# Two units of the RWKV5 attention go over to the 64-step form, and the 64-step form turns its blocks before it moves them

## The chip, the core and the metric

The kernel runs on one core of one Trainium2 chip. The core has a matrix engine (PE, TensorE), a vector engine (DVE, VectorE), a scalar engine (ACT), a general engine (POOL, GpSimd) and an engine that here only issues DMAs (SP, SyncE). Each engine takes its instructions in program order and waits for the others by semaphores. The metric is the device time of one execution in microseconds (us), the median of three timed runs.

## The reference

Batch 4, 8 heads, 768 steps, head dimension 48. An RWKV5 attention runs over the steps; its output, seen as 3072 tokens of 384 values, feeds a SwiGLU feed-forward block with 1536 hidden values.

```python
for t in range(S):
    kt, vt, rt = (k[:, :, t], v[:, :, t], r[:, :, t])
    cur = np.einsum('bhd,bhe->bhde', u[None] * kt, vt)
    y[:, :, t] = np.einsum('bhd,bhde->bhe', rt, state + cur)
    state = w[None, :, :, None] * state + np.einsum('bhd,bhe->bhde', kt, vt)
...
g = x @ w_gate
silu = g * (1.0 / (1.0 + np.exp(-g)))
val = x @ w_val
return (silu * val @ w_out)
```

## The kernel before

The attention is cut into 24 units of 128 rows. A unit `i` is either one batch and 128 steps (below `PAIRED`, here 0 to 9) or a pair of batches with 64 steps each (10 to 23). In a unit POOL scales k and r by powers of w (`scale_k`, `scale_r`) into slots of one large tile, `hats`. The scaled k and r must then be turned, so that the head dimension lies along the partitions, for the scores (k by r within the unit). `outputs` multiplies the masked scores (tile `At`, with the own term of u on the diagonal) by v and adds what the state of the earlier steps gives; `update` adds the unit's k by v to the state. `At` gets its masked scores from VectorE, by predicated copies.

*128-step units* are turned by TensorE: eight transposes of 128x128 into PSUM (`turn`, L415), which ACT copies to tiles `kT` and `rT`. Then come eight matmuls of scores (L508), the outputs (L659) and the update (L672); VectorE adds the update to the state `zs` (L684) and POOL multiplies that by w.

*64-step units* are turned without TensorE. `move_blocks` issues eight DMAs on SP (L445), which bring 32x32 blocks of `hats` to their partitions in slots 6 and 7 of `hats`, in runs of 32 values (128 bytes). Two transposes by VectorE (`turn_block`, L467), which turn each block of 32x32 within itself, then write `kT` and `rT`. Scores (L560) and outputs (L594) work on halves of 64 rows; the state lies beside v in `v_ld`, and two DMAs by SP (`fill_turned`, L538) bring the turned r into `At` for the outputs, and two by ACT (`fill_own`) the own term. `paired_update` (L608) comes right behind the scores of the next unit.

A loop over stages `s` sets the order. In stage s: POOL scales unit s + 1, units below 10 are turned, the scores of unit s − 1 come, and the outputs of unit s − 2 with their update: ahead of the scores for 64-step units, behind them for the last 128-step units (`LATE`). `after_visit` lists VectorE's small work of a 64-step stage in the deque `lazy`: masked copies, the own term, the two transposes of unit s, and the additions to the state. In the second transpose's step also stand the scaling of r and the moves of unit s + 1, the fills and the loads of unit s + 3. So the moves of a unit are issued a stage ahead of its transposes.

Between these, `gaps(s, n)` puts pieces of other work at five places of a stage, n from 0 to 4. From stage 12 they are pieces of the feed-forward block, as many as `share` says. In stages 4 to 11 the table `EARLY` lists them: `F` is a `feed`, one piece of the feed-forward block (there a gate group, `gate_value`, L705: six matmuls of 128x256 that serve two units, then a sigmoid on ACT and a product on VectorE, L712) with up to three steps of `lazy`. `R` is a `round_weights`: ACT and VectorE round a chunk of the weights (L214, L229), POOL completes it, and SP loads another chunk of 768 KB into `w_bits` (L194). Two PSUM banks serve the gate groups in turn, and two the rounding.

```python
    EARLY = {s: ("" if s < 7 else "R", "F", "R", "F", "RF") for s in range(5, 12)}
    EARLY[10] = ("", "FF", "RR", "F", "RF")
    EARLY[11] = ("R", "FF", "R", "F", "RF")
```

The loads, the moves and the fills stand on SP's one queue in program order, and each DMA there takes its turn on one of eight completion semaphores.

## Time and profile before

| | |
|---|---|
| median of 3 timed runs | 580.44 us (580.26 to 580.53) |
| the profiled execution | 579.8 us |
| its span on the core | 578.0 us |
| granted TensorE clock | 0.998 |
| instructions in the span | 13726 |

The profile's page gives the busy time of each engine, then 40 slices of the span, the DMA queues, the chain of work that ended last, and groups of instructions. The prediction quotes the lines that it uses. TensorE's row in the 40 slices reads 9 (90% or more) in all but the first and the last:

```profile
PE   8999999999999999999999999999999999999996
DVE  8887887299497699497789597878268787477772
DMA  8999895544544516534425534310200000200002
```

A row of a timeline has start, duration, engine, line, operation, out<-in, shapes and count. TensorE's rows count each float32 matmul of the program twice (a gate group of six reads x12), its transposes once.

### The profile page before, as it was taken

The page shows a single profiled execution, that of the slowest core. Times are in us where ns is not written, and L with a number is a line of the kernel's source. Part 1 is how long each engine was busy: PE and PEld are TensorE (multiplying, and loading weights), DVE is VectorE, ACT ScalarE, POOL GpSimd, SP SyncE. Part 2 cuts the span into 40 slices and gives each one's busy share as a digit, 9 for nine tenths or more (in the row PEclk, how much of TensorE's full clock was granted, in tenths as well). Part 3 has the DMA queues.
Part 4 walks back from the last instruction along what each step waited for, and adds up shares of the span by engine and source line. Part 5 has one row for each costly group of instructions (what it writes and reads, how often), then busy time and mean ns, then how long its engine had stood idle before and what let it go on. Part 6 is the DMA issues. An engine that isn't in the chain of part 4 may idle for free.

```text
span 578.0 us, 13726 instructions
## 1 busy us (share of the span) xinstructions
PE 569.0 (98%) x5424; PEld 512.8 (89%) x5424; DVE 428.4 (74%) x753; ACT 223.2 (39%) x532; POOL 394.4 (68%) x395
## 2 busy tenths in 40 slices
PE   8999999999999999999999999999999999999996
PEld 7788888899878899988899988899988899888896
DVE  8887887299497699497789597878268787477772
ACT  3768887222344432353521344421233320234310
POOL 6889898998999818979527979528988950010700
PEclk9999999999999999999999999999999999999999
DMA  8999895544544516534425534310200000200002
GB/s 203 239 262 260 229 238 113 113 70 102 106 84 84 95 29 127 109 64 94 77 40 105 120 69 78 56 35 20 56 1 0 1 1 2 54 2 0 2 1 59
DMA packets 152663, 49.16 MB, mean 85 GB/s; under 512 B 139729, under 2 KB 142802, under 8 KB 152594
## 3 DMA queue, kind: packets, MB, share of 16 engines
q1 hardware_dynamic: 147794, 41.22, 34.1%
q10 hardware_dynamic: 4800, 7.02, 4.4%
q8 instruction: 44, 0.72, 0.5%
q14 instruction: 25, 0.20, 0.1%
HBM read 28.31 MB, written 4.72 MB: 57 GB/s over the span
## 4 chain that ended last, share of the span: by engine, by line
PE 93%; POOL 2%; DMA 1%; SPq 1%; DVE 1%; issue 1%; ACT 0%; DVEq 0%; POOLq 0%
PE bank L974 30%; PE bank L785 18%; PE ring L974 13%; PE bank L705 11%; PE bank L1207 8%; PE ring L659 3%; PE ring L594 2%; PE ring L560 2%; PE ring L508 2%; PE ring L1207 1%; PE ring L415 1%; PE ring L608 1%; SPq L445 1%; DMA hats<-in_r_dram 1%; POOL rk L274 1%
## 5 line engine op out<-in xcount | busy, mean ns | idle before, releaser
L998 DVE TENSOR_TENSOR hv<-hv,bank 128x512 f32<-128x512 f32 x132 | 87.7, 683 | 40.4 <-PE bank L974 34.8
L705 PE MATMUL bank<-xT,wgv 128*128 128x256 f32 x288 | 66.2, 384 | 0.2 <-ACT xT L663 0.2
L974 PE MATMUL bank<-xf,wgv 128*128 128x256 f32 x256 | 65.8, 381 | 0.1
L998 ACT COPY hv<-bank 128x512 f32<-128x512 f32 x72 | 40.8, 584 | 58.8 <-PE bank L974 56.8
L705 PEld LDWEIGHTS bank<-xT,wgv 128*128 128x128 f32 x288 | 53.4, 190 | 8.2 <-ACT xT L663 0.4
L974 PEld LDWEIGHTS bank<-xf,wgv 128*128 128x128 f32 x256 | 47.9, 190 | 7.2 <-DVE kT L1252 0.6
L1261 POOL TENSOR_TENSOR hv<-At,hats 128x512 f32<-128x512 f32 x8 | 10.2, 1276 | 63.7 <-ACT At L1260 63.7
L1005 ACT ACTIVATE hv<-hv 128x512 f32<-128x512 f32 (+2 forms) x36 | 22.8, 633 | 52.8 <-DVE hv L998 52.8
L974 PE MATMUL bank<-xT,wgv 128*128 128x256 f32 x144 | 35.8, 381 | 0.0
L974 PE MATMUL bank<-xT,s 128*128 128x256 f32 x152 | 35.2, 379 | 0.0
L386 ACT ACTIVATE zs<-mask,du 128x64 f32<-128x64 f32 x96 | 29.6, 346 | 11.9 <-DVE hv L798 6.2
L785 PE MATMUL bank<-wt,hs 128*128 128x192 f32 x192 | 34.1, 328 | 0.0
L785 PE MATMUL bank<-wo,hs 128*128 128x192 f32 x192 | 33.9, 327 | 0.0
L762 POOL TENSOR_TENSOR hs<-hv,hs 128x768 f32<-128x768 f32 x6 | 11.2, 1872 | 32.3 <-DVE hs L759 32.3
L974 PEld LDWEIGHTS bank<-xT,s 128*128 128x128 f32 x152 | 28.8, 190 | 4.2 <-issue 0.3
L785 PE MATMUL bank<-wo,hv 128*128 128x192 f32 x192 | 32.5, 326 | 0.0
L904 POOL TENSOR_TENSOR s<-s,wgv 128x256 f32<-128x256 f32 x39 | 30.1, 772 | 2.9
L785 PEld LDWEIGHTS bank<-wo,hs 128*128 128x128 f32 x192 | 31.7, 190 | 0.4 <-DVE hv L793 0.3
L904 POOL TENSOR_TENSOR s<-wgv 128x256 f32<-128x256 f32 x39 | 30.1, 790 | 2.8 <-PE bank L785 2.8
L785 PEld LDWEIGHTS bank<-wo,hv 128*128 128x128 f32 x192 | 31.6, 190 | 0.4
L904 POOL TENSOR_TENSOR s<-s 128x256 f32<-128x256 f32 x39 | 31.4, 805 | 0.8
L785 PEld LDWEIGHTS bank<-wt,hs 128*128 128x128 f32 x192 | 31.4, 190 | 0.2
(238 smaller groups left out, 1435.4 us busy)
## 6 DMA issues: line engine op xcount, KB each, us to landing
hats<-hats SPq DMA_DIRECT2D x112, 64.0 KB, 2.4
w_bits<-in_moe_w_gate_dram SPq DMA_DIRECT2D x6, 768.0 KB, 7.0
w_bits<-in_moe_w_val_dram SPq DMA_DIRECT2D x6, 768.0 KB
w_bits<-in_moe_w_out_dram SPq DMA_DIRECT2D x6, 768.0 KB, 7.8
At<-rT SPq DMA_DIRECT2D x28, 128.0 KB, 4.1
At<-zs ACTq DMA_DIRECT2D x24, 128.0 KB, 2.4
k_ld<-in_k_dram SPq DMA_DIRECT2D x28, 96.0 KB, 3.9
r_ld<-in_r_dram SPq DMA_DIRECT2D x28, 96.0 KB, 3.4
```

The costliest lines, as they stand in the source:

```text
L386: lambda h=h: act.activation(own_of(i)[:, slot(i, h), :], ident64, AF.Identity, scale=du[:, h : h + 1])
L508: pe.matmul(ps[e][:, a, :], kT[i % 2][rows, at(i, a), :], turned[i][rows, at(i, a), :], start=True, stop=True, skip_group_check=True,)
L560: pe.matmul(ps[p][o : o + 64, n, :], kt[rows, n + HP * g, :], rT[rows, n + HP * g, :], start=True, stop=True, skip_group_check=True,)
L594: pe.matmul(ps[32 * q : 32 * q + 32, cc, 64 * p : 64 * p + 64], *x, start=start, stop=stop, skip_group_check=True,)
L659: pe.matmul(ps[32 * q : 32 * q + 32, cc, :], *x, start=start, stop=stop, skip_group_check=True,)
L705: pe.matmul(gv[:, o, :].rearrange("p (i t) -> p i t", i=2), wt[:, c, P * f : P * (f + 1)], xT[:, 2 * g % NX : 2 * g % NX + 2, c, :], start ...
L785: pe.matmul(ps, lhs[:, f, :], rhs[:, f, :], start=(f == 0 and n in (0, 1, 4)), stop=(f == FH - 1), skip_group_check=True,)
L904: op(made[o], made[a], made[b])
L974: pe.matmul(ps[:, o], u[:, o], v, start=first and o == 0, stop=True, skip_group_check=True,)
L998: do(out, *(pair_of(wide[a][:]) if isinstance(a, str) else a for a in args))
L1005: todo.append((at, lambda: act.activation(gate, gate, AF.Silu)))
L1207: pe.matmul(ps, (h[what][q] if h[what] is D_ else h[what][:, q])[:, f, :], wide["o"][what][:, f, :], start=first and f == 0 and (split or ...
```

## The change

`PAIRED` goes from 10 to 8, so units 8 and 9 become 64-step units; all 16 of them now take their batches and steps by one formula. In every 64-step unit the two steps of the turning change places. VectorE first turns the 32x32 blocks of k and of r, with four transposes that write `blocks` (slots 6 and 7 of `hats`), two heads interleaved element by element. Eight DMAs on SP (L437 of the changed kernel) then move the blocks in runs of 64 values (256 bytes) into a tile `kr`, which the scores read: k and r of one head are every second element there. `At` and the own term take the same interleaved form. The moves of unit s now belong to stage s, and the fills (L517) of unit s − 1 come behind its scores. `scale_r` of unit s + 1 moves to the front of stage s. `EARLY` changes in stages 8 and 10, and in stages 8 to 11 the transposes stand at the front of `lazy`. The reordered slots of heads (`at`, `slot`), the form with moved blocks for 128-step units (`BLOCKS`), and `late` go.

```diff
--- before.py
+++ after.py
...
@@ -120,13 +120,18 @@
     hats = cst.tile([P, 8, H, 64], FP32, name="hats")
     khat, rhat = [hats[:, n] for n in (0, 2, 3, 5)], [hats[:, n] for n in (1, 4)]
     At = [cst.tile([P, H, P], FP32, name=f"At{i}") for i in range(2)]
-    kT = [cst.tile([P, HP, P], FP32, name=f"kT{i}") for i in range(2)]
-
-
-    blocks = [hats[:, n].rearrange("p h x -> p (h x)") for n in (7, 6)]
+    both_turned = [cst.tile([P, 2 * HP * P], FP32, name=f"kr{i}") for i in range(2)]
+    parts = [t[:] for t in both_turned]
+    parts.append(cst.tile([P, HP * P], FP32, name="kr2")[:])
+    parts = [t[:, 512 * n : 512 * n + 512] for t, n in zip(parts + parts[1::-1], (0, 0, 0, 1, 1))]
+    kT = [t.rearrange("p (a t) -> p a t", a=HP) for t in parts[0:2]]
+    rT_of = [parts[n].rearrange("p (a t) -> p a t", a=HP) for n in (3, 2, 4)]
+
+
+    blocks = hats[:, 6:8].rearrange("p n h x -> p (n h x)")
 
     def rhat_of(i):
-        return rhat[i % 2 if i < BLOCKS else i % 4 // 2]
+        return rhat[i % 2]
...
-    PAIRED = 10
+    PAIRED = 8
 
     def part(i, p):
 
-        if i < PAIRED + B // 2:
-            return 2 + p, PAIRED // B * P + 64 * (i - PAIRED)
-        c, q = divmod(i - PAIRED - B // 2, 2)
-        return 2 * q + p, (PAIRED // B + 1) * P + 64 * c
+        c, q = divmod(i - PAIRED, 2)
+        return 2 * q + p, PAIRED // B * P + 64 * c
 
...
+    def in_pairs(x):
+
+        return x.rearrange("p h t -> p (h t)").rearrange("p (a t e) -> p a e t", a=HP, e=2)
+
     def diagonal(i, on_act=None):
 
         du = dus.pop(i)
         if i >= PAIRED:
             small.extend(
                 lambda h=h: act.activation(
-                    own_of(i)[:, slot(i, h), :], ident64, AF.Identity, scale=du[:, h : h + 1]
+                    in_pairs(own_of(i))[:, h // 2, h % 2], ident64, AF.Identity,
+                    scale=du[:, h : h + 1],
                 )
                 for h in range(H)
             )
@@ -409,7 +409,7 @@
     def turn(i):
         kr = khat[i % 4], rhat_of(i)
         tps = [next_psum(HP, P) for _ in kr]
-        turned[i] = three.tile([P, HP, P], FP32, name="rT", tag="rT")
+        turned[i] = rT_of[i % 3]
         for tp, t, dst, table in zip(tps, kr, (kT[i % 2], turned[i]), (pw[:, :, 1 : P + 1], pv)):
             for a in range(HP):
                 pe.transpose(tp[:, a, :], pair(t, a), ident[:])
@@ -418,62 +418,29 @@
             else:
                 act.copy(dst[:], tp[:])
 
+    def turn_block(i, n):
+
+        src = (khat[i % 4], rhat_of(i))[n].rearrange("p (a e) (b x) -> p b a e x", b=2, e=2)
+        dst = blocks.rearrange("p (b n a j e) -> p b n a e j", b=2, n=2, a=HP, e=2)
+        for b in range(2):
+            dve.transpose(dst[:, b, n], src[:, b])
+
     def move_blocks(i):
 
...
-    def turn_block(i, n):
-
-        if n == 0:
-            turned[i] = three.tile([P, HP, P], FP32, name="rT", tag="rT")
-        dst = (kT[i % 2], turned[i])[n]
-        if i < PAIRED:
-            merged = hats[:, 6:8].rearrange("p n h x -> p (n h x)").rearrange(
-                "p (q n a x) -> p n q a x", q=4, n=2, a=HP
-            )
-            dve.transpose(dst[:].rearrange("p a (t q) -> p q a t", q=4), merged[:, n])
-        else:
-            dve.transpose(dst[:].rearrange("p a t -> p (a t)"), blocks[n])
+                    o = 64 * p + 32 * m
+                    sp.dma_start(out=dst[q : q + 32, m], in_=src[o : o + 32, b])
 
     def after_visit(s):
 
         def turn_second():
             turn_block(s, 1)
-            if s + 1 < N:
-                scale_r(s + 1)
-                move_blocks(s + 1)
-            fill_turned(s)
+            move_blocks(s)
             if s + 3 < N:
                 load(s + 3)
 
@@ -482,17 +449,20 @@
             diagonal(s + 1)
 
         masked, sums = list(lazy)[:4], list(lazy)[4:]
-        if len(masked) < 4:
-            masked = [*masked, *(lambda: None for _ in range(4 - len(masked)))]
+        turns = [lambda: turn_block(s, 0), turn_second]
+        mine = [own_term] if s + 1 < N else []
         lazy.clear()
-        ahead = sums if s == PAIRED + 2 else []
-        lazy.extend([
-            *ahead, *masked[:2], own_term if s + 1 < N else lambda: None,
-            lambda: turn_block(s, 0), masked[2], turn_second, masked[3],
-            *(sums if not ahead else []),
-        ])
-        while s == PAIRED and lazy:
-            lazy.popleft()()
+        if s in EARLY:
+            lazy.extend(turns + masked + mine + sums)
+            if s < PAIRED + 2:
+                lazy.append(lambda: hand_over(s - 2))
+            lazy.append(lambda: load_v(s))
+            for _ in range(2 if s == PAIRED else 0):
+                lazy.popleft()()
+        else:
+            lazy.extend([
+                *masked[:2], *mine, turns[0], masked[2], turns[1], masked[3], *sums,
+            ])
 
     lazy = deque()
 
...
@@ -527,26 +496,37 @@
     def both(i):
 
         return At[i % 2][:].rearrange("p h t -> p (h t)").rearrange(
-            "p (o h t) -> p o h t", o=2, h=H
+            "p (o a t e) -> p o a e t", o=2, a=HP, e=2
         )
 
+    def half_of(i, p):
+
+        return At[i % 2][:].rearrange("p h t -> p (h t)")[:, 512 * p : 512 * p + 512]
+
+    def turned_of(i, n):
+
+        return both_turned[i % 2][:].rearrange(
+            "p (n a t e) -> p n a e t", n=2, a=HP, e=2
+        )[:, n]
+
     def fill_turned(i):
 
-        rT = turned[i][:].rearrange("p a (e t) -> p (a e) t", e=2)
+        rT = both_turned[i % 2][:, 4 * P : 8 * P]
         for p in range(2):
             there = slice(64 - 64 * p, P - 64 * p)
-            sp.dma_start(out=both(i)[there, p], in_=rT[there])
+            sp.dma_start(out=half_of(i, p)[there], in_=rT[there])
 
...
     def paired_scores(i, ps):
 
-        rT = turned.pop(i)[:].rearrange("p a (e t) -> p (a e) t", e=2)
-        kt = kT[i % 2][:].rearrange("p a (e t) -> p (a e) t", e=2)
+        kt, rT = [turned_of(i, n) for n in range(2)]
         sums = [
             x.rearrange("p a t -> p (a t)")[:, 256 : 256 + HP * D]
             .rearrange("p (h d) -> p h d", h=HP) for x in reversed(ps)
@@ -558,14 +538,17 @@
                 for g in range(2):
                     o = 64 * (p ^ g)
                     pe.matmul(
-                        ps[p][o : o + 64, n, :], kt[rows, n + HP * g, :], rT[rows, n + HP * g, :],
+                        ps[p][o : o + 64, n, :], kt[rows, n // 2 + 2 * g, n % 2], rT[rows, n // 2 + 2 * g, n % 2],
                         start=True, stop=True, skip_group_check=True,
                     )
 
         def masked_copy(p, g):
             rows, o = slice(64 * p, 64 * p + 64), 64 * (p ^ g)
-            m = mask64[rows].bitcast(INT32).unsqueeze(1).to_broadcast([64, HP, 64])
-            dve.copy_predicated(both(i)[rows, p, HP * g : HP * g + HP], m, ps[p][o : o + 64])
+            m = mask64[rows].bitcast(INT32).unsqueeze(1).unsqueeze(1)
+            dve.copy_predicated(
+                both(i)[rows, p, 2 * g : 2 * g + 2], m.to_broadcast([64, 2, 2, 64]),
+                ps[p][o : o + 64].rearrange("p (a e) t -> p a e t", e=2),
+            )
 
         for p in range(2):
             for g in range(2):
...
@@ -1358,8 +1338,7 @@
                 coming = 40 * ((s < 14) + (s < 18)) + 14 * (s < 22)
                 share[0] = -(-(len(todo) + coming) // max(25 - s, 1))
             feed(
-                share[0] // 5 + (n < share[0] % 5) - (n == 1 and BLOCKS <= s < PAIRED),
-                1,
+                share[0] // 5 + (n < share[0] % 5), 1,
             )
             return
         for what in EARLY[s][n]:
@@ -1369,13 +1348,13 @@
                 elif len(summed) < 4:
                     weight_sum()
             else:
-                feed(1, 3, 2)
+                feed(1, 3, 3)
 
     share = [0]
-    BLOCKS = 10
-    LATE = 10
+    LATE = 8
     EARLY = {s: ("" if s < 7 else "R", "F", "R", "F", "RF") for s in range(5, 12)}
-    EARLY[10] = ("", "FF", "RR", "F", "RF")
+    EARLY[8] = ("R", "F", "", "F", "RF")
+    EARLY[10] = ("R", "FF", "RR", "F", "RF")
     EARLY[11] = ("R", "FF", "R", "F", "RF")
     EARLY[4] = ("R", "F", "", "F", "F")
 
@@ -1475,17 +1454,13 @@
             own_sum(s)
         if s == PAIRED:
             diagonal(s)
-        late = BLOCKS < s + 1 < N and s % 2 == 0
-        if s + 1 == BLOCKS:
-            turn(s)
         if s + 1 < N:
             scale_k(s + 1)
-            if s < PAIRED and not late:
-                scale_r(s + 1)
+            scale_r(s + 1)
             own_product(s + 1)
-            if s + 1 < BLOCKS:
+            if s + 1 < PAIRED:
                 load_v(s + 1)
-        if s + 1 < BLOCKS:
+        if s < PAIRED:
             turn(s)
         gaps(s, 0)
         if s > N:
@@ -1503,34 +1478,17 @@
                 outputs(s - 2)
                 update(s - 2)
                 fill_own(s)
-            if s > PAIRED + 1 and s < N:
-                if s == PAIRED + 2:
-                    load_v(s - 1)
-                load_v(s)
+            if s > PAIRED:
+                fill_turned(s - 1)
             if PAIRED <= s < N:
+                if s not in EARLY:
+                    load_v(s)
                 after_visit(s)
-            if s == PAIRED:
-                hand_over(s - 2)
-                load_v(s)
-            if s == PAIRED + 1:
-                hand_over(s - 2)
             gaps(s, 1)
-        if BLOCKS <= s < PAIRED:
-            turn_block(s, 0)
-            feed(1)
-            turn_block(s, 1)
-        if late and s < PAIRED:
-            scale_r(s + 1)
+        gaps(s, 2)
         if s + 2 == PAIRED:
             sp.dma_start(out=scales[64:P, 1:3], in_=scales[0:64, 1:3])
-        if BLOCKS <= s + 1 <= PAIRED:
-            move_blocks(s + 1)
-            if s + 1 < PAIRED:
-                load_v(s + 1)
-        if late and s < PAIRED:
-            load(s + 3)
-        gaps(s, 2)
-        if s < PAIRED and not late:
+        if s < PAIRED:
             load(s + 3)
         if s + 1 == PAIRED:
 
```

Three places in the order of the instructions. First SP's queue before the change, around the moves of unit 10 (`hats<-hats`; `w_bits` are weight chunks, `k_ld` and `r_ld` the loads of later units, `v_ld<-zs` hands a state over):

```order
L194 DMA w_bits<-in_moe_w_out_dram 128x2x768
L157 DMA k_ld_104<-in_k_dram 64x8x48 x2
L157 DMA r_ld_102<-in_r_dram 64x8x48 x2
L692 DMA v_ld_107<-zs 48x4x48 x2
L194 DMA w_bits<-in_moe_w_out_dram 128x2x768
L445 DMA hats<-hats 32x16x32 x8
L157 DMA k_ld_103<-in_k_dram 64x8x48 x2
```

The changed kernel, around the moves of unit 8 and of unit 9 (`kr<-hats`; `At<-kr` are the fills of unit 8):

```order
L197 DMA w_bits<-in_moe_w_out_dram 128x2x768 x2
L437 DMA kr_112<-hats 32x8x64 x8
L160 DMA k_ld_104<-in_k_dram 64x8x48 x2
L160 DMA r_ld_102<-in_r_dram 64x8x48 x2
L675 DMA v_ld_107<-zs 48x4x48 x2
L166 DMA v_ld_105<-in_v_dram 64x4x48 x2
L166 DMA v_ld_106<-in_v_dram 64x4x48 x2
L197 DMA w_bits<-in_moe_w_out_dram 128x2x768 x2
L517 DMA At_110<-kr_112 64x512 x2
L437 DMA kr_113<-hats 32x8x64 x8
```

The last two weight loads, with loads and a hand-over ahead of them, now stand between the moves of unit 8 and those of unit 9.

Second, VectorE in the changed kernel from the last rounding ahead of unit 8's transposes (L426; L486 are masked copies of unit 7, L667 additions to the state of unit 6):

```order
L232 TENSOR_SCALAR wo<-bank_95 128x384
L233 SCALAR_TENSOR_TENSOR wo<-bank_95,wo 128x384
L486 COPY_PREDICATED At_111<-mask,ring_98 128x4x128
L486 COPY_PREDICATED At_111<-mask,ring_99 128x4x128
L667 TENSOR_TENSOR zs<-ring_97,zs 48x4x48 x2
L426 STREAM_TRANSPOSE hats<-hats 128x4x2x32 x4
L695 TENSOR_TENSOR hv<-sgs,bank_93 128x256
```

and a stage on, around the transposes of unit 9 (L695 are products of gate groups, L548 masked copies of unit 8):

```order
L667 TENSOR_TENSOR zs<-ring_97,zs 48x4x48 x2
L695 TENSOR_TENSOR hv<-sgs,bank_92 128x256
L426 STREAM_TRANSPOSE hats<-hats 128x4x2x32 x4
L548 COPY_PREDICATED At_110<-mask,ring_98 64x2x2x64
L232 TENSOR_SCALAR wo<-bank_94 128x384
```

The four transposes of a unit, where before there were two behind the moves, stand ahead of the product of a gate group in the first place and behind one in the second.

Third, TensorE around the turning and the scores of unit 8, before (L705 a gate group, L415 the transposes, L508 the scores):

```order
L705 MATMUL bank_92<-xT,wgv 128x256 x6
L705 MATMUL bank_93<-xT,wgv 128x256 x6
L415 MATMUL ring_96<-ident,hats 128x128 x4
L415 MATMUL ring_97<-ident,hats 128x128 x4
L508 MATMUL ring_98<-rT,kT_112 128x128
```

and in the changed kernel (L655 the update of unit 6, L688 gate groups, L540 the scores of unit 8):

```order
L655 MATMUL ring_97<-v_ld_107,hats 32x48 x16
L688 MATMUL bank_93<-xT,wgv 128x256 x6
L688 MATMUL bank_92<-xT,wgv 128x256 x6
L688 MATMUL bank_93<-xT,wgv 128x256 x6
L540 MATMUL ring_98<-kr_112 64x64 x2
```

The transposes are gone from TensorE, and three gate groups stand between the update of unit 6 and the scores of unit 8.

59 lines of the change are left out of this document (14 added, 45 removed).

## The prediction

> **What bounds the kernel now.** I read the busy shares first, then the chain of work that ended last, then what TensorE waited for.
>
> ```profile
> PE 569.0 (98%) x5424; PEld 512.8 (89%) x5424; DVE 428.4 (74%) x753; ACT 223.2 (39%) x532; POOL 394.4 (68%) x395
> PE 93%; POOL 2%; DMA 1%; SPq 1%; DVE 1%; issue 1%; ACT 0%; DVEq 0%; POOLq 0%
> ```
>
> TensorE is busy for 569.0 of the 578.0 us span, and 93% of the last chain is TensorE. Its recorded waits on other engines are these:
>
> ```profile
> PE ring L316 <- POOL ident masks.py:199: 1.5, 1, 1.5
> PE ring L659 <- DVE At L516: 1.0, 3, 0.6
> PE ring L608 <- issue: 0.5, 1, 0.5
> PE bank L705 <- ACT xT L663: 0.2, 1, 0.2
> ```
>
> 1.5 + 1.0 + 0.5 + 0.2 = 3.2 us, half of it once at the start. So almost nothing is left to gain by shortening waits. A change can gain by taking matmuls off TensorE, and it loses whenever TensorE meets data that are late. This change does both, so each is priced.
>
> **Term 1: TensorE work that goes.** Units 8 and 9 leave the 128-step form and join the 64-step form. The timeline of TensorE, with start, duration and count, shows one 128-step unit. Matmuls overlap, so I take start to start:
>
> ```profile
> 83.88 1.04 PE L415 MATMUL ring<-ident,hats 128*128 128x128 f32 x8
> 84.85 1.16 PE L508 MATMUL ring<-rT,kT 48*128 48x128 f32 x16
> 85.94 2.86 PE L705 MATMUL bank<-xT,wgv 128*128 128x256 f32 x12
> 88.72 0.43 PE L659 MATMUL ring<-rT,zs 112*32 112x128 f32 x8
> ...
> 90.29 0.52 PE L672 MATMUL ring<-v_ld,hats 128*32 128x48 f32 x32
> 90.74 1.56 PE L705 MATMUL bank<-xT,wgv 128*128 128x256 f32 x6
> ```
>
> The transposes take 84.85 − 83.88 = 0.97, the scores 85.94 − 84.85 = 1.09, the outputs 90.29 − 88.72 = 1.57 and the update 90.74 − 90.29 = 0.45: 4.08 us in all. A 64-step unit, later on:
>
> ```profile
> 148.00 1.11 PE L594 MATMUL ring<-At,v_ld 112*32 112x64 f32 x64
> 149.04 0.69 PE L560 MATMUL ring<-rT,kT 48*64 48x64 f32 x32
> 149.55 0.63 PE L608 MATMUL ring<-v_ld,hats 64*64 64x48 f32 x32
> 150.11 1.13 PE L974 MATMUL bank<-xf,s 128*128 128x256 f32 x4
> ```
>
> That is 1.04 + 0.51 + 0.56 = 2.11 us. Two units save 2 × (4.08 − 2.11) = **−3.9 us**, the whole gain that the change can bring.
>
> **Term 2: the new wait ahead of the scores.** Before, the eight moves of a 64-step unit were issued a stage early, and only two VectorE transposes stood between the blocks and the scores. Now VectorE transposes first, the eight moves follow, and the scores read what the moves wrote. The moves in steady state, and their entry among the DMA issues (KB each, median us from issue to landing):
>
> ```profile
> 214.08 5.39 SPq L445 DMA_DIRECT2D hats<-hats  x8
> ...
> hats<-hats SPq DMA_DIRECT2D x112, 64.0 KB, 2.4
> ```
>
> One issue takes 5.39 / 8 = 0.67 us, so the last starts 7 × 0.67 = 4.7 us after the first and lands 2.4 later: **7.1 us from the first move to usable data**. The first moves read the first 32-row halves of both k and r, so they need three of the four transposes. The eight moves have as many bytes as before in half as many runs; I keep their issue and landing times. The price of a transpose of 256 elements is not in the trace. The nearest row is that of 512:
>
> ```profile
> L467 DVE STREAM_TRANSPOSE rT<-hats 128x512 f32<-128x512 f32 x14 | 9.9, 704 | 0.1
> L712 DVE TENSOR_TENSOR hv<-sgs,bank 128x256 f32<-128x256 f32 x24 | 10.0, 415 | 13.1 <-ACT sgs L711 13.0
> L711 ACT ACTIVATE sgs<-bank 128x256 f32<-128x256 f32 x24 | 9.1, 380 | 21.6 <-PE bank L705 21.6
> ```
>
> It lies between half of 0.704, 0.35, and the whole, 0.70; an elementwise operation on 256 takes 0.415, so I take 0.38. Three are 1.1 us.
>
> *Unit 8.* Its stage starts where before the transposes of unit 8 started:
>
> ```profile
> 66.45 5.45 PE L705 MATMUL bank<-xT,wgv 128*128 128x256 f32 x24
> 71.73 1.04 PE L415 MATMUL ring<-ident,hats 128*128 128x128 f32 x8
> ...
> 74.84 0.56 DVE L229 TENSOR_SCALAR wo<-bank 128x384 int32<-128x384 int32 x1 [0.61 <-ACT bank L214]
> ...
> 77.16 1.39 DVE L516 COPY_PREDICATED At<-mask,ring 128x512 f32<-128x512 int32 x2
> ...
> 80.93 0.73 DVE L684 TENSOR_TENSOR zs<-ring,zs 48x192 f32<-48x192 f32 x2
> ```
>
> The trace has two rows for each matmul of the gate groups, so these 24 are two groups of six matmuls, and a group is (71.73 − 66.45) / 2 = 2.64 us. From 71.73 TensorE now runs scores, outputs and update of older units (1.09 + 1.57 + 0.45), and is at 74.84; three gate groups bring it to 82.8, where the scores of unit 8 stand. VectorE has the weight rounding to 77.16, two masked copies to 78.5, two state additions of 0.73 to 79.2, then the transposes: third done at 80.3, data landed at 80.3 + 7.1 = 87.4. **Wait 4.6 us.** If ACT released the rounding 2.3 us earlier, so that all of VectorE's list moved up by 77.16 − 74.84, and the third gate group waited 1.7 us for its bank, which the first group's product behind the transposes frees, 0.6 would be left; if the rounding came 1.9 us later, 6.5.
>
> *Unit 9.* Its transposes stand behind the product of that stage's first gate group. From the start of unit 8's scores: 0.51 + 1.57 + 0.45 + 2.64, then 0.38 and 0.415 for activation and product, and 1.1, are 7.1; with the moves 14.2. TensorE has 0.51 + 1.57 + 0.45 + 3 × 2.64 + 1.04 = 11.5 before the scores of unit 9. So 2.7 us are missing even with empty queues. They are not empty: two 768-KB weight loads stand ahead of these moves on SP, which before stood one or two stages away from them.
>
> ```profile
> 84.19 0.55 SPq L194 DMA_DIRECT2D w_bits<-in_moe_w_out_dram  x1
> 86.29 6.09 SPq L445 DMA_DIRECT2D hats<-hats  x8
> 92.48 1.32 SPq L157 DMA_DIRECT2D k_ld<-in_k_dram  x2
> ...
> w_bits<-in_moe_w_out_dram SPq DMA_DIRECT2D x6, 768.0 KB, 7.8
> ...
> hats<-hats SPq DMA_DIRECT2D x8, 64.0 KB, 3.4
> ```
>
> Before, the moves that were issued 2.1 us behind one such load took 6.09 instead of 5.39 us to issue and 3.4 instead of 2.4 to land. With two loads of 7.8 us just ahead I charge two to four us more: wait 5 to 7 us, taken as **6.0**. [...]
>
> *Units 10 and 11.* Unit 10 has two more groups of gate work and its weights have landed: 0.4 us (0 to 1). Unit 11 has gate and projection work of over 14 us ahead of its scores: nothing.
>
> *Units 12 to 23.* VectorE's order there stays as it was, so the slack of before can be read: from the end of the second transpose to the scores.
>
> ```profile
> 213.31 0.71 DVE L467 STREAM_TRANSPOSE rT<-hats 128x512 f32<-128x512 f32 x1
> ...
> 219.88 1.11 PE L594 MATMUL ring<-At,v_ld 112*32 112x64 f32 x64
> 220.93 0.84 PE L560 MATMUL ring<-rT,kT 48*64 48x64 f32 x30
> ```
>
> 220.93 − 214.02 = 6.9 us here, one of the three tightest of twelve. The need from that point is 7.1 less a transpose, since the first moves go when the third of four is done: 6.7. So 0 to 0.3 each in the tight ones: **0.5** together, 0 at best, 3 if each of the twelve missed by a quarter.
>
> **Costed at nothing, and what covers it.** VectorE gets 64 transposes of 0.38 for 28 of 0.704: 24.3 − 19.7 = 4.6 us more on an engine that is 74% busy; it costs at most those 4.6 if all of it fell ahead of moves. Copies and diagonals of units 8 and 9 on ACT, at 39%, and the earlier scaling of r on POOL have other work ahead of TensorE. The fills of At go out a little later on SP and are needed a stage on; they stand ahead of the next moves, and each issue is 0.67 us or more, which is in the 6.0. TensorE now reads every second element as operands. No row here shows a strided read; it lies between nothing and a doubling of the scores and outputs: (0.51 + 1.04) × 16 units = 25 us. I take nothing, by the nearest row, L560 above: the same matmul of 64x64 with its operands side by side. [...]
>
> **Sum.** −3.9 + 4.6 + 6.0 + 0.4 + 0.5 = +7.6 us on the profiled execution of 579.8, whose span is 578.0 with 1.8 around it: 587.4. The median of the timed runs, 580.44, lies 0.6 above the profiled one, within what runs differ, so I say **587.5**.
>
> **Rivals.**
> - *The waits stay at their structural least.* 0.6 and 2.7 with the rest 0: −3.9 + 3.3 = −0.6, or 579.8, the same. If the groups of unit 9 also spread so far that its moves are hidden, only the −3.9 is left: 576.5, faster. For it: all queues but TensorE have idle time. Against it: a 7.1 us chain against a stage of 11.5, whose first 6 us must pass before VectorE may transpose. It decides where both waits together fall under 2.7 us.
> - *The weights do not delay the moves of unit 9.* 2.7 instead of 6.0: 584.
> - *Strided operands cost.* From +3 to +25 us on top: 590 to 612. Against it stands only that no wait or row speaks for it.
> - *The order of VectorE in steady state slips*, so that each of twelve units waits 1 us: 587.5 + 11.5 = 599. Against it: the slack rows.
> - *The change does not take the TensorE work away*, as the 64-step form could run slower beside gate groups than in the later stages: at most the 3.9 again, 591.
>
> **How the numbers follow.** About 0.2% of this time, 1.16 us, is what a measurement can tell from no change. Forecast, 585.5 to 590: 0.45. Weights harmless, or one of the waits short, 581.7 to 585.5: 0.22. All waits short: 0.25, of which 0.15 faster and 0.10 the same. Above 590 by strides, slipping or lost saving: 0.08. So faster 0.15, same 0.10, slower 0.75. The range from 578.0 to 592.0 leaves out some 0.08 below and 0.07 above.
>
> **What would show it.** TensorE's busy time 4 us lower. In its waits a row of the 64-step scores waiting for the DMAs of kr, some 4 to 7 us each in two instances around 80 to 110 us, and almost nothing later. On VectorE, transposes of 256 elements near 0.38 us. On SP, moves of unit 9 issued behind two weight loads, landing later than 2.4. Scores of 32 matmuls still at 0.51 and outputs at 1.04. Waits under 2.7 us together, or a matmul that got slower, would make the forecast wrong.

## The result, and the profile after

| | before | changed kernel |
|---|---|---|
| median of the timed runs | 580.35 us (580.0 to 580.53) | 610.34 us (609.88 to 612.21, 4 runs) |
| ratio | | 1.0524 [1.05, 1.0547] |
| span of the profiled execution | 578.0 us | 609.1 us |
| mean granted TensorE clock | 0.998 | 0.980 |

The kernel became slower by 5.2%, as forecast in sign, but by 30 us where 7 were forecast. The page of the changed kernel, first the busy times, then the row of the granted clock in 40 slices, then the shares of the chain that ended last:

```profile
PE 580.0 (95%) x5456; PEld 519.8 (85%) x5456; DVE 453.8 (75%) x797; ACT 220.6 (36%) x528; POOL 396.0 (65%) x395
PEclk9999998789989999999999989999999999999999
PE 71%; DVE 13%; DMA 5%; ACT 4%; issue 3%; SPq 3%; POOL 1%; DVEq 0%; POOLq 0%
```

TensorE's share of the chain fell from 93% to 71%. Its idle time rose from 578.0 − 569.0 = 9.0 to 609.1 − 580.0 = 29.1 us, by **20.1**; its busy time rose by **11.0**, where 3.9 us less was forecast. Together they are the 31.1 us of the span. Where they lie shows in the windows of both kernels (window, then busy time and count of TensorE, weight loads, VectorE, ACT and POOL, then granted clock, DMA share, GB/s), before:

```profile
60.00:160.00 100.00, 100.00 (x1210) 89.91 (x1209) 71.94 (x133) 49.34 (x136) 92.05 (x88) 1.00 0.62 139
160.00:470.00 310.00, 309.21 (x2878) 278.53 (x2877) 238.18 (x396) 108.87 (x251) 237.16 (x244) 1.00 0.33 62
```

and the changed kernel:

```profile
60.00:160.00 100.00, 85.36 (x1024) 75.35 (x1023) 68.10 (x128) 39.76 (x114) 71.42 (x60) 0.91 0.61 141
160.00:470.00 310.00, 303.70 (x2939) 273.04 (x2939) 243.28 (x411) 104.78 (x250) 231.63 (x250) 0.99 0.32 69
```

Between 60 and 160 us TensorE idles 14.6 us, and the mean granted clock there is 0.91. The largest waits of the whole span, by what ended them (total us, times, longest; "issue" is a wait for nothing that the profile shows), and the early ones on TensorE's timeline (the bracket is the idle time ahead of the row):

```profile
PE ring L540 <- DMA kr<-hats: 9.4, 5, 2.8
PE ring L577 <- DVE At L548: 3.3, 2, 2.9
PE ring L540 <- issue: 2.8, 3, 1.5
PE bank L688 <- DVE hv L695: 1.8, 1, 1.8
PE bank L768 <- DVE hs L742: 1.8, 1, 1.8
```

```profile
82.59 2.86 PE L688 MATMUL bank<-xT,wgv 128*128 128x256 f32 x12 [1.84 <-DVE hv L695]
...
87.92 0.34 PE L540 MATMUL ring<-kr 48*64 48x64 f32 x4 [2.47 <-DMA kr<-hats]
89.36 0.70 PE L540 MATMUL ring<-kr 48*64 48x64 f32 x28 [1.10 <-DMA kr<-hats]
...
104.59 0.44 PE L577 MATMUL ring<-At,v_ld 112*32 112x64 f32 x8 [2.94 <-DVE At L548]
105.36 2.05 PE L577 MATMUL ring<-At,v_ld 128*32 128x64 f32 x56 [0.33 <-DVE At L548]
...
108.80 1.01 PE L540 MATMUL ring<-kr 48*64 48x64 f32 x26 [0.98 <-DMA kr<-hats]
...
127.67 0.54 PE L540 MATMUL ring<-kr 48*64 48x64 f32 x21 [2.84 <-DMA kr<-hats]
...
140.85 1.38 PE L768 MATMUL bank<-wt,hs 128*128 128x192 f32 x7 [1.79 <-DVE hs L742]
...
172.53 1.01 PE L540 MATMUL ring<-kr 48*64 48x64 f32 x26 [2.04 <-DMA kr<-hats]
```

Unit 8 thus waited 1.84 + 2.47 + 1.10 = 5.4 us, unit 9 2.94 + 0.33 + 0.98 = 4.25, unit 10 2.84, unit 11 1.79 (a projection), unit 12 2.04; the row "issue" holds 1.55 at the scores of unit 20 and 1.00 at those of unit 16. The outputs of 56 matmuls at 105.36 take 2.05 us; at full clock 64 take 1.17 (the row at 221.86, further down).

A second view of the loss is how late a unit's outputs start (the first row of L577 for each unit, of L594 in the kernel before), since TensorE keeps its order. The last three columns are versions told of further down:

| outputs of unit | before, us | changed kernel | pool_late | old_form_8b | new_form_10b |
|---|---|---|---|---|---|
| 10 | 127.17 | +19.7 | +14.7 | +13.4 | +1.4 |
| 12 | 172.78 | +24.6 | +19.4 | +17.2 | +5.9 |
| 16 | 262.82 | +25.6 | +18.4 | +15.9 | +5.6 |
| 20 | 351.58 | +29.8 | +20.5 | +15.9 | +7.6 |
| 23 | 413.40 | +31.3 | +21.9 | +16.0 | +8.8 |

So in the changed kernel some 25 us are lost by unit 12 and 6.7 more behind it.

### The profile page after: what moved, and what is told of

It is laid out like the page before. It is cut to its first block, busy times and chain, and to the rows that moved or that the text cites. A ratio compares the mean times of both kernels' runs of the same rounds, so it can differ in the third digit from the quotient of the medians.

```text
span 609.1 us, 13940 instructions
## 1 busy us (share of the span) xinstructions
PE 580.0 (95%) x5456; PEld 519.8 (85%) x5456; DVE 453.8 (75%) x797; ACT 220.6 (36%) x528; POOL 396.0 (65%) x395
## 3 DMA queue, kind: packets, MB, share of 16 engines
q1 hardware_dynamic: 123922, 42.79, 31.1%
## 4 chain that ended last, share of the span: by engine, by line
PE 71%; DVE 13%; DMA 5%; ACT 4%; issue 3%; SPq 3%; POOL 1%; DVEq 0%; POOLq 0%
PE bank L957 23%; PE bank L768 13%; PE ring L957 12%; PE bank L1190 8%; PE bank L688 5%; DVE hv L981 3%; DVE At L548 3%; DMA kr<-hats 3%; PE ring L577 2%; PE ring L540 2%; SPq L437 1%; DVE hats L426 1%; PE ring L591 1%; PE ring L1190 1%; DMA At<-hv 1%
## 5 line engine op out<-in xcount | busy, mean ns | idle before, releaser
L688 PE MATMUL bank<-xT,wgv 128*128 128x256 f32 x288 | 69.5, 398 | 2.1 <-DVE hv L695 1.8
L688 PEld LDWEIGHTS bank<-xT,wgv 128*128 128x128 f32 x288 | 56.2, 200 | 11.1 <-DVE hv L695 2.2
L548 DVE COPY_PREDICATED At<-mask,ring 64x256 f32<-64x256 int32 x64 | 46.6, 728 | 2.4 <-PE ring L591 1.3
L610 POOL TENSOR_TENSOR v_ld<-v_ld,w 48x384 f32<-48x384 f32 x28 | 27.5, 983 | 30.9 <-DVE v_ld L607 22.8
L385 ACT ACTIVATE zs<-mask,du 128x64 f32<-128x64 f32 x96 | 30.1, 351 | 24.6 <-DVE du L288 9.4
L957 PE MATMUL bank<-xT,wgv 128*128 128x256 f32 x144 | 35.6, 380 | 0.1
L887 POOL TENSOR_TENSOR s<-s 128x256 f32<-128x256 f32 x39 | 33.1, 848 | 1.0
L768 PEld LDWEIGHTS bank<-wt,hs 128*128 128x128 f32 x192 | 31.3, 190 | 2.7 <-issue 2.1
```

What stands on the lines that cost most here:

```text
L385: lambda h=h: act.activation(in_pairs(own_of(i))[:, h // 2, h % 2], ident64, AF.Identity, scale=du[:, h : h + 1],)
L548: dve.copy_predicated(both(i)[rows, p, 2 * g : 2 * g + 2], m.to_broadcast([64, 2, 2, 64]), ps[p][o : o + 64].rearrange("p (a e) t -> p a e ...
L610: pool.tensor_mul(ze, ze, w.unsqueeze(3).to_broadcast([D, HP, 2, D]))
L688: pe.matmul(gv[:, o, :].rearrange("p (i t) -> p i t", i=2), wt[:, c, P * f : P * (f + 1)], xT[:, 2 * g % NX : 2 * g % NX + 2, c, :], start ...
L768: pe.matmul(ps, lhs[:, f, :], rhs[:, f, :], start=(f == 0 and n in (0, 1, 4)), stop=(f == FH - 1), skip_group_check=True,)
L887: op(made[o], made[a], made[b])
```

## The experiments

Two theories stood against each other. By the one, the loss is set by the chain through VectorE, SP and POOL: transposes, moves, masked copies, roundings. By the other, a good part is the granted clock, which falls behind TensorE's waits, so that a wait costs more than it lasts. Beside them stood the parts: the 64-step form from unit 8, the new order of turning, and the small edits costed at nothing. Each kernel was timed in three rounds; medians of before in the same rounds were 578.87 to 579.82.

**old_form_8: units 8 and 9 in the old form.** Before, with the 64-step form from unit 8, but blocks moved first and transposed after.

```diff
-    PAIRED = 10
+    PAIRED = 8
...
-    BLOCKS = 10
-    LATE = 10
+    BLOCKS = 8
+    LATE = 8
...
-    EARLY[10] = ("", "FF", "RR", "F", "RF")
+    EARLY[8] = ("R", "F", "", "F", "RF")
+    EARLY[10] = ("R", "FF", "RR", "F", "RF")
```

> The kernel before with PAIRED, BLOCKS and LATE at 8, the batches of the units and the rounding table of the changed kernel, but with the old order of turning (moves a stage early, then two transposes). If the reversed order of turning is what costs, TensorE gets its 3.9 us back and nothing new waits: about 576.5 us, TensorE busy near 565, almost no waits, clock near 1. If the early 64-step units themselves cost (short stages, weight loads beside the moves), the time stays above 590, with waits of the scores of units 8 and 9.

Measured 603.16 us, ratio 1.0399 [1.0373, 1.0425]. One wait carries more than half of it. The waits of TensorE, and the row of VectorE behind it:

```profile
PE ring L592 <- DVE At L566: 13.7, 1, 13.7
```

```profile
106.53 0.56 DVE L227 TENSOR_SCALAR wo<-bank 128x384 int32<-128x384 int32 x1 [10.83 <-ACT bank L212]
```

The outputs of unit 8 waited for masked copies that stand behind a rounding, and that rounding 10.83 us for a weight load. The outputs of unit 10 come 23.5 us late, those of unit 23 25.6: behind unit 12 (26.6) this order loses nothing.

**new_form_10: the new order alone.** The changed kernel with units 8 and 9 of 128 steps again.

```diff
-    PAIRED = 8
+    PAIRED = 10
...
-    LATE = 8
+    LATE = 10
...
-    EARLY[8] = ("R", "F", "", "F", "RF")
-    EARLY[10] = ("R", "FF", "RR", "F", "RF")
+    EARLY[10] = ("", "FF", "RR", "F", "RF")
```

> The changed kernel with the first 64-step unit at 10 again, and the batches and rounding table of before: the reversed order of turning alone. If the loss is made in stages 8 to 10, where the stage is short, most of it goes: 583 to 590. If the reversed form costs in every unit (56 masked copies at 0.728 instead of 0.443 us, 16 us of VectorE, and the waits from unit 11 on, 10.7 us in the changed kernel), 592 to 600.

Measured 597.74 us, 1.0322 [1.0283, 1.0361]. Here the loss grows along the program: 2.8 us at unit 10, 6.0 at 12, 13.3 at 16, 17.4 at 23. So the new order, with the small edits that came with it (the slower masked copies and POOL's earlier scaling of r), costs 17 us over units 10 to 23, where the prediction had 0.9 (unit 10 and units 12 to 23).

**mask_flat: masked copies with adjacent writes.** The interleaved form lets a masked copy write every second element of `At`. VectorE's groups, before and changed (the pairs are busy us and mean ns):

```profile
L568 DVE COPY_PREDICATED At<-mask,ring 64x256 f32<-64x256 int32 x56 | 24.8, 443 | 1.1
```

```profile
L548 DVE COPY_PREDICATED At<-mask,ring 64x256 f32<-64x256 int32 x64 | 46.6, 728 | 2.4 <-PE ring L591 1.3
```

A copy takes 728 ns instead of 443. The edit swaps the order of the elements, so that the writes lie side by side and the reads of PSUM step.

```diff
-            m = mask64[rows].bitcast(INT32).unsqueeze(1).unsqueeze(1)
+            m = mask64[rows].bitcast(INT32).unsqueeze(1).unsqueeze(3)
             dve.copy_predicated(
-                both(i)[rows, p, 2 * g : 2 * g + 2], m.to_broadcast([64, 2, 2, 64]),
-                ps[p][o : o + 64].rearrange("p (a e) t -> p a e t", e=2),
+                both(i)[rows, p, 2 * g : 2 * g + 2].rearrange("p a e t -> p a t e"),
+                m.to_broadcast([64, 2, 64, 2]),
+                ps[p][o : o + 64].rearrange("p (a e) t -> p a t e", e=2),
             )
```

> The changed kernel with its masked copies in the order that writes neighbouring elements one after the other and reads PSUM in steps of 64 elements. If the step of two elements in what is written makes a copy 0.728 instead of 0.443 us, it goes back to about 0.44 and the waits for it (2.9 us at the outputs of unit 8, and those behind a late VectorE in stages 11 to 20, some 6 us, with the slower clock behind them) go: 595 to 602. If any step, read or written, costs the same, the copies stay near 0.73 and the time near 610.

```profile
L548 DVE COPY_PREDICATED At<-mask,ring 64x256 f32<-64x256 int32 x64 | 28.3, 441 | 1.1
```

The copies are back at 441 ns, 18.3 us less on VectorE, and the time is 611.33 us, 1.0544 [1.0523, 1.0564]: unchanged. The slow copies were real, and taking them away alone gained nothing: the waits went over to `kr`, 15.2 us in seven, and VectorE's 55 sums of 128x256 took 51 us in all where they took 42 in the changed kernel, half of what the copies had saved.

**busy_waits: matmuls in the waits.** 5 to 16 matmuls of the identity, whose results nobody reads, ahead of the scores of three units and the outputs of one, so that TensorE is busy while it would wait.

```diff
+                if s == 10:
+                    warm(14, ring_a[0])
                 outputs(s - 2)
...
+            if s in (9, 10, 11):
+                warm({9: 16, 10: 5, 11: 14}[s], ring_a[0])
             scores(s - 1)
```

> The changed kernel with 49 matmuls on the identity, whose results nobody reads, put into TensorE's waits ahead of the scores of units 8, 9 and 10 and the outputs of unit 8. If a wait costs a second time because the granted clock falls behind it (0.50 to 0.83 in the 4 us slices between 88 and 132 us), the clock stays near 1, and the matmuls behind the waits run at their old pace: 600 to 605 us though TensorE has more to do. If the clock has another cause, the time stays at 610 or rises by what the 49 take, to 614.

Measured 610.65 us, 1.0539 [1.0496, 1.0582]. The clock stayed at 1.00 from 84 to 96 us, and the outputs of unit 10 were 16.1 us late instead of 19.7. But at units 16 and 20 it was 25.8 and 30.0, as in the changed kernel. The test was not clean: the filling matmuls ahead of the outputs of unit 8 themselves waited for a bank that masked copies read.

**gap_cost: what a wait costs where TensorE is the bound.** Before, with five waits put in between units 12 and 22: TensorE waits for a chain of n small copies on ACT.

```diff
+    WAITS = {13: 2, 15: 5, 17: 9, 19: 14, 21: 20}
...
+    def wait_for_act(n):
+
+        ps = ring_a[0][:, 0:1]
+        pe.matmul(ps, ident[:], ident[:, 0:1], start=True, stop=True)
+        act.copy(sg0[:], ps)
+        for _ in range(n):
+            act.copy(sg0[:], sg0[:])
+        pe.matmul(ps, ident[:], sg0[:], start=True, stop=True)
...
+        if s in WAITS:
+            wait_for_act(WAITS[s])
```

> The kernel before, with one artificial wait of TensorE in each of the stages 13, 15, 17, 19 and 21: a matmul, a chain of 3, 6, 10, 15 and 21 tiny copies on ACT behind it, and a matmul that needs the last; nothing else changes. [...] If a wait costs only itself, the time is 580 + 11.4 = 592 and the granted clock stays at 1. If the granted clock falls behind longer waits, as it did in the changed kernel (2.4 us more at unit 20 for a wait of 1.55), 598 to 605, and the clock rows behind the longer waits show 0.5 to 0.8.

Measured 611.96 us, 1.0551 [1.0529, 1.0573]. The profiled execution took 616.74 us, and its span is 614.9 − 578.0 = 36.9 us longer than before for waits that sum to 22.5; the 11.4 us of the expectation were a guess that no run shows. The waits of TensorE, and two windows behind the first of them, which ended at 162.57:

```profile
PE ring L1390 <- ACT sg L1389: 22.5, 5, 6.1
```

```profile
163.40:165.40 2.00, 2.00 (x6) 1.55 (x6) 0.29 (x1) 0.00 (x0) 2.00 (x4) 0.50 0.47 86
...
169.40:171.40 2.00, 2.00 (x11) 1.77 (x10) 1.01 (x2) 1.96 (x6) 1.92 (x3) 1.00 0.42 64
```

The granted clock is 0.50 until 169.12, 6.55 us behind the wait, and there are six rows of matmuls in 2 us instead of eleven. Behind the other four waits it is 0.50 for 5.85, 5.69, 3.41 and 5.39 us. Stage by stage the waits of 3.62, 4.14, 3.08, 6.15 and 5.54 us cost 6.55, 6.75, 6.47, 8.41 and 8.79: 2.3 to 3.4 us each on top of themselves. Some 0.5 us of that is not the clock but, by the estimate from gap_short below, the inserted matmuls.

**pool_late: the scaling of r back to its old place.** Mask_flat, with POOL's `scale_r` from stage 12 on behind the moves again, as before.

```diff
             move_blocks(s)
+            if s > 11 and s + 1 < N:
+                scale_r(s + 1)
...
-            scale_r(s + 1)
+            if s <= 11:
+                scale_r(s + 1)
```

> The kernel with the contiguous masked copies (mask_flat, 611.3), in which from stage 12 on POOL scales r of the next unit as late as in the kernel before, behind the moves of this unit instead of at the front of the stage. If the waits at units 16 and 20 come from POOL's row moving by 1 us, so that its sums and VectorE's sums meet in memory and VectorE's transposes come 2.6 us later against the scores (slack 4.9 instead of 7.5 us), both waits go and the time falls by 6 to 9 us, to 602 to 605. If the waits are the length of the chain itself, they stay: 610.

Measured 601.72 us, 1.0403 [1.0353, 1.0453]: 9.6 us less than mask_flat by the medians and some 8 by the ratios, the largest gain of any one edit. VectorE's row of mask_flat near unit 16, what POOL did then, and the same two sums in pool_late:

```profile
249.28 1.57 DVE L915 TENSOR_TENSOR sgs<-xT 128x256 f32<-128x256 f32 x1
250.89 2.98 DVE L915 TENSOR_TENSOR xT<-xT 128x256 f32<-128x256 f32 x1
```

```profile
251.51 2.08 POOL L888 TENSOR_TENSOR s<-wgv 128x256 f32<-128x256 f32 x3
```

```profile
245.99 0.58 DVE L917 TENSOR_TENSOR sgs<-xT 128x256 f32<-128x256 f32 x1
246.60 0.42 DVE L917 TENSOR_TENSOR xT<-xT 128x256 f32<-128x256 f32 x1
```

The same instruction takes 2.98 us beside POOL's sums and 0.42 where POOL stands idle; the transposes of unit 16 stand behind it. In the changed kernel the two rows take 1.57 and 1.92 us. The outputs of unit 9, ahead of the first stage that the edit touches, start at 122.17 in pool_late and 122.24 in mask_flat; those of unit 10 at 141.91 and 144.83, those of unit 23 at 435.31 and 446.67. Of the first 2.9 us, 1.8 are a shorter wait of the scores of unit 10 (1.00 against 2.83), which still stand ahead of the edited stage, so not all of the difference is the edit's. All 55 sums take 39 us before, 42 in the changed kernel, 51 in mask_flat and 46 in pool_late: the price was measured beside the flat masked copies, and how much of it the changed kernel pays is not shown. Whether it was the stretched sums alone or also POOL's own results coming later was not separated.

**weights_act: the last weight loads on another queue.** Two loads of 768 KB stood ahead of the moves of unit 9 on SP; here ACT issues the last four loads.

```diff
-            sp.dma_start(
+            (act if n >= NW - 4 else sp).dma_start(
```

> The changed kernel with the last four weight loads on ACT's queue instead of SP's. By the prediction the loads ahead of the moves of unit 9 cost some 3 us there; by the trace they come late on SP behind the hand-over, and the rounding that waits for them holds the masked copies of unit 8 (2.9 us at its outputs). If either holds, the wait at the outputs of unit 8 goes and unit 10's outputs come 4 to 8 us earlier: 602 to 607. If the loads are only as late as their buffers, 610.

Measured 608.16 us, 1.0513 [1.0471, 1.0555], which the total cannot tell from the changed kernel. The profile can: the wait at the outputs of unit 8 fell from 2.94 + 0.33 to 0.80 + 0.45 + 0.22 us, and the outputs of unit 10 were 16.4 us late instead of 19.7. The moves of unit 9 went out in 5.29 us instead of 7.89. So some 3 us are the weights in this pair of executions; as the four runs spread from 604.76 to 612.07 and the profiled one is the fastest, the size is rough.

**old_form_8b: the old form without its 13.7 us wait.** old_form_8 with the same loads on ACT, and the masked copies at the front of VectorE's small work.

```diff
+        if s in EARLY:
+            lazy.extend(masked + [own_term, lambda: turn_block(s, 0), turn_second] + sums)
```

> old_form_8 (603.2) with the masked copies ahead of the transposes in stages 9 to 11 and the last four weight loads on ACT's queue. Its wait of 13.7 us at the outputs of unit 8 stood behind a rounding that waited 10.8 us for a weight load, which stood behind hand-over and loads of v on SP. If that is all that keeps the old order of turning from earning its 3.9 us, the wait goes and with it the slow clock behind it: 577 to 585. If early 64-step units need more than the stage has, other waits take its place and it stays above 590.

Measured 595.53 us, 1.0256 [1.0218, 1.0295]. The long wait went; a new one came at an earlier place, where a gate group waits for its bank behind a rounding that waits for the weights, 6.1 us.

Even the old order of turning loses 13 to 17 us with units 8 and 9 in the 64-step form, all of it before unit 12.

**moves_split: the moves over two queues.** pool_late with every second move issued by ACT.

```diff
-                    sp.dma_start(out=dst[q : q + 32, m], in_=src[o : o + 32, b])
+                    on = act if m else sp
+                    on.dma_start(out=dst[q : q + 32, m], in_=src[o : o + 32, b])
```

> pool_late (601.7) with every second of the eight moves of a unit issued on ACT's queue instead of SP's. The last move is then issued after 3 instead of 7 spacings of 0.67 us, so the data are there 2.7 us earlier. If the length of the chain makes the waits of the scores (2.9, 1.9, 1.0, 2.6 and 1.5 us at units 8, 9, 10, 12 and 20 in pool_late), nearly all of them go, with the slow clock behind them: 590 to 595. If ACT, which waits in order for the transposes, delays its own work as much, or the moves are late for another reason, 600 or more.

Measured 611.79 us, 1.0562 [1.0541, 1.0583]: 10 us worse than pool_late. The scores hardly wait any more (once, 0.75 us at unit 10, which the profile puts down to an addition of VectorE's), but ACT's own work and the masked copies come late instead:

```profile
PE bank L961 <- ACT hv L985: 8.3, 3, 2.9
PE ring L581 <- DVE At L551: 4.9, 1, 4.9
```

**pool_late_busy and new_form_8b: the clock again, more cleanly.** pool_late with filling matmuls, once also ahead of the outputs of unit 8, once (with the weights on ACT too) only ahead of the scores of units 8, 9, 10 and 12.

```diff
+                if s == 10:
+                    warm(14, ring_a[0])
                 outputs(s - 2)
...
+            if s in (9, 10, 11, 13):
+                warm({9: 14, 10: 8, 11: 8, 13: 10}[s], ring_a[0])
             scores(s - 1)
```

> pool_late (601.7) with 54 matmuls on the identity, whose results nobody reads, in TensorE's waits: ahead of the scores of units 8, 9, 10 and 12 and of the outputs of unit 8. The waits stay as long, only filled; if each of them costs 2 to 3 us more by the slow clock behind it, as in the kernel with artificial waits, four or five such costs of 1.5 to 3 us go: 592 to 598. If the clock is not what costs, the time stays at 601 to 603.

> pool_late (601.7) with the last four weight loads on ACT's queue (3.3 us at unit 10 in weights_act) and with 40 matmuls on the identity ahead of the scores of units 8, 9, 10 and 12, none ahead of the outputs of unit 8, where those of pool_late_busy stood behind the masked copies and ran after the wait, not in it. If the late weights and the clock behind the waits of the scores are separate costs, 3.3 and some 5 us go: 592 to 596. If the early stages are as long as their chain of weights, rounding and masked copies whatever TensorE does, 599 to 603.

They measured 602.88 us, 1.0391 [1.0367, 1.0414], and 601.57 us, 1.0384 [1.0361, 1.0406]; pool_late had 1.0403. The mean clock rose from 0.982 to 0.993 and 0.992, and the time stayed. In pool_late_busy the fill ahead of the outputs again waited for the masked copies (5.9 us). In new_form_8b none did, so this is the cleanest answer: in stages 8 to 12 the time is set by the chain, whatever TensorE's clock is meanwhile. It has two edits, though, and what the filling matmuls themselves cost was not separated. The outputs of unit 9 came 3.9 us earlier than in pool_late (118.26 against 122.17), and those of unit 10 no earlier (142.30 and 141.91). The chain of unit 10 there, VectorE's transposes and then SP's queue:

```profile
111.35 1.42 DVE L426 STREAM_TRANSPOSE hats<-hats 128x256 f32<-128x256 f32 x4
```

```profile
107.60 4.47 SPq L678 DMA_DIRECT2D v_ld<-zs  x2
...
116.16 6.27 SPq L437 DMA_DIRECT2D kr<-hats  x8
```

The blocks were ready at 112.8; the moves went out from 116.16 on, behind the hand-over of a state, four loads of v and two fills on the same queue: 3.4 us. That these could stand behind the moves was not tried.

**new_form_10b: the best of the new order.** new_form_10 with the edits of mask_flat and pool_late.

> new_form_10 (597.7) with the contiguous masked copies and the late scaling of r: the reversed order of turning alone, without its two avoidable costs. If those two made the waits at units 11, 15, 16 and 20 and the slow matmuls behind them, only the chain's own wait at unit 12 is left, some 2.5 us with 2.5 us of slow clock: 582 to 586. If the reversed order costs in itself, it stays at 592 or more.

Measured 588.66 us, 1.0156 [1.0139, 1.0173]: 9 us better than new_form_10, and still 9 slower than before. Its largest wait is none of the moves':

```profile
PE ring L583 <- POOL v_ld L616: 3.4, 1, 3.4
```

The last addition to the state, now at the end of VectorE's list of a stage, ended at 149.56, and POOL's product behind it, which the outputs of unit 11 read, stood behind three other instructions and came at 152.44.

**gap_short: where the clock falls.** gap_cost with eleven short waits.

```diff
-    WAITS = {13: 2, 15: 5, 17: 9, 19: 14, 21: 20}
+    WAITS = {s: 0 for s in range(12, 23)}
```

> The kernel before with a short artificial wait in each of the stages 12 to 22: a matmul, one tiny copy on ACT and a matmul that needs it (as in gap_cost, without the chain). What ACT has queued ahead decides each wait, so some 0.5 to 3 us each, 11 of them. If a wait costs double only from some length on, those under about 1.8 us (in the changed kernel 1.79 and 1.84 were followed by a clock of 1, 1.55 and 2.04 in the scores by 0.5) cost themselves alone and the clock stays at 1 behind them, and longer ones are followed by some 3 us at 0.5. If every wait has its share, the clock falls a little behind each, and the time rises by about 1.6 times the sum of the waits.

Measured 606.52 us, 1.0477 [1.0458, 1.0496], for 16.7 us of waits. Nine of them, 0.59 to 2.24 us long, left the clock at 1.00. Two were 3.02 us long; behind the first it stayed, behind the second it fell. Their rows on TensorE, and the window behind each:

```profile
216.06 0.38 PE L1390 MATMUL ring<-sg,ident 128*128 128x1 f32 x2 [3.02 <-ACT sg L1387]
...
313.74 0.58 PE L1390 MATMUL ring<-sg,ident 128*128 128x1 f32 x2 [3.02 <-ACT sg L1387]
```

```profile
216.00:218.00 2.00, 1.94 (x12) 1.94 (x13) 1.97 (x4) 0.00 (x1) 0.00 (x0) 1.00 0.00 0
...
314.00:316.00 2.00, 2.00 (x8) 2.00 (x9) 2.00 (x3) 0.00 (x0) 0.13 (x1) 0.50 0.00 0
```

The first cost its stage 2.8 us, the second 6.8. The span is 603.7 − 578.0 = 25.7 us longer, so the other ten waits, 13.7 us in all, cost 18.9: about 0.5 us each on top of themselves, an estimate of what the inserted matmuls cost (their two rows take 0.28 and 0.38 us).

No version is faster than the kernel before; the nearest, new_form_10b, keeps units 8 and 9 in the 128-step form.

## Why the prediction had the sign and missed the size

**Where the sum failed.** Up to the outputs of unit 10 the prediction's terms make −3.9 + 4.6 + 6.0 + 0.4 = 7.1 us, and those outputs came 19.7 late; behind them it had 0.5, and 31.3 − 19.7 = 11.6 came. TensorE's account shows which terms are missing. Between 20 us and the outputs of unit 10 it idles (126.87 − 111.48) − (107.17 − 106.16) = 14.4 us more than before; the waits of units 8 to 10, forecast at 11.0, are 12.7 of that. It is busy for 15.5 us at a clock of 0.50 (90.66 to 94.07, 104.31 to 114.55, 128.20 to 131.62), which loses half, 7.7 us. 14.4 + 7.7 − 3.9 = 18.2. From there to unit 23 it idles 5.6 us more and loses 3.4 us of clock. So the waits that were priced one by one came out near; the steps that failed are those put at nothing or next to it: the clock behind the waits, and the waits of units 11 to 23, with the new order of VectorE and POOL that makes them. The account says where TensorE's time went, not what would win it back.

**Term 1, −3.9 us: no run disproves it, and no time shows it alone.** The transposes of two units are gone from TensorE's rows (80 to 64). But a saving on TensorE counts only where TensorE sets the time, and in stages 8 to 12 it ceased to.

**Unit 8, 4.6 us: right.** 5.4 were measured, of which 1.84 at the bank of a gate group, the place that the prediction named for its better case. The moves went out at 81.79 and the last scores ran at 89.36: 7.6 us, where 7.1 was worked out.

**Unit 9, 6.0 us: 4.25 came, and mostly at another place.** The charge for the weights was right for the moves themselves:

```profile
95.69 1.06 SPq L197 DMA_DIRECT2D w_bits<-in_moe_w_out_dram  x2
...
98.38 7.89 SPq L437 DMA_DIRECT2D kr<-hats  x8
```

From the first move to the last scores at 108.80 it is 10.4 us, 3.3 more than the 7.1 worked out, where two to four were charged. But only 0.98 us of wait was left at the scores, since TensorE was late itself: 3.27 us came ahead of the outputs of unit 8, which the prediction did not have. VectorE's row shows why:

```profile
98.60 0.68 DVE L548 COPY_PREDICATED At<-mask,ring 64x256 f32<-64x256 int32 x1
101.09 0.56 DVE L232 TENSOR_SCALAR wo<-bank 128x384 int32<-128x384 int32 x1 [1.81 <-ACT bank L217]
...
103.80 2.27 DVE L548 COPY_PREDICATED At<-mask,ring 64x256 f32<-64x256 int32 x3
```

One masked copy of unit 8 stood ahead of the roundings, three behind, and the rounding waited for its weight load. So the weights delayed VectorE's list as well as the moves; old_form_8 shows the same, with 10.83 us. This order of VectorE was quoted ahead of the prediction, which priced only the moves in it.

**Unit 10, 0.4 us: 3.0 came** (2.84 + 0.20). The step "its weights have landed" looked at the weights alone. What stands ahead of the moves on SP, a hand-over, four loads and two fills, was counted for unit 9 and not here, though each issue there took 0.60 to 0.69 us (114.02 to 120.09).

**Units 12 to 23, 0.5 us: 11.6 came behind unit 10.** Alone, with units 8 and 9 in the 128-step form, the new order of turning costs 17.4 us over units 10 to 23 (new_form_10), 8.8 in its best form (new_form_10b). Three things failed in this term. First, "one of the three tightest of twelve" was read from too few rows: in the kernel before, the second transpose of unit 12 stood here,

```profile
143.77 0.71 DVE L467 STREAM_TRANSPOSE rT<-hats 128x512 f32<-128x512 f32 x1
```

and its scores began at 149.04, a slack of 4.6 us, with 6.7 needed. The forecast of this row alone would be 2.1; measured 2.04. That is in part luck: in new_form_10 and new_form_10b TensorE waits over 3 us for the state ahead of these scores, and they then wait for no move. Second, the earlier scaling of r on POOL, "costed at nothing" because POOL has other work ahead of TensorE, stretched VectorE's sums ahead of the transposes of unit 16; taking it back gained 8 to 10 us (pool_late against mask_flat), with what is said there left open. Third, the masked copies were not priced at all (285 ns more for each); alone they turned out to be worth nothing, and together with POOL's order they were not taken apart.

**Not in the sum: the clock.** No term had it. By the mean clock TensorE lost 609.1 × 0.020 = 12.2 us against 578.0 × 0.002 = 1.2 before. Yet the runs do not show it as a cause of its own in stages 8 to 12: new_form_8b gave most of it back and gained nothing, as a slow TensorE there fills time in which it would wait. Where TensorE is the bound, gap_cost shows it as a cost: waits of 3.1 to 6.2 us cost 6.5 to 8.8. Of the 6.7 us behind unit 12 it makes 1.7 by the account: the stretch of 0.50 from 356.90 to 360.31.

**The rivals.** *Strided operands cost* names a range, 590 to 612, in which the time fell, and has no part in it. A 64-step unit with its operands two elements apart, at full clock:

```profile
221.86 1.17 PE L577 MATMUL ring<-At,v_ld 112*32 112x64 f32 x64
...
224.11 1.13 PE L957 MATMUL bank<-sgs,wgv 128*128 128x256 f32 x4
```

224.11 − 221.86 = 2.25 us, against 2.11 before: 0.14 × 16 = 2.2 us in all, estimated from this one unit. The forecast's bound of 25 took a doubling of 0.51 + 1.04 us, which no run shows. *The order of VectorE in steady state slips*, 599, was the right rival, with a chance far too small; together with the early stages it is the result.

In order of size, by unit 23, and roughly, since old_form_8b has two edits more: about 16 us for units 8 and 9 in the 64-step form (old_form_8b, old order), about 9 for the new order at its best (new_form_10b), which together are 24.8 where pool_late, with both, has 21.9; and 31.3 − 21.9 = 9.4 for POOL's earlier scaling of r and the slow masked copies, of which the latter alone gained nothing. What of the first 16 could be had back by another order of SP and VectorE stays open.

## What to carry to other kernels

When a change takes work off the engine that sets the time and hands it to a chain over others, list the slack of every instance of the new chain, not of a typical one, and write down everything that stands ahead of it on each queue it passes: here the unit that was not looked at, the hand-over on SP and the roundings on VectorE each took 2 to 3 us. Moving an instruction on an engine with much idle time is not free if it then runs beside the work of another engine that it slows down: here a sum on VectorE took 2.98 us beside POOL's sums in mask_flat, and 0.42 in pool_late, where POOL stood idle. And a wait of the engine that sets the time can cost more than it lasts (in gap_cost 3.08 us cost 6.47, and 6.15 cost 8.41): test fills and shorter chains apart, since giving the clock back gained nothing here while the chain was the bound.
